# A gated attention and state-space kernel: rebuilding its set-up (parameters, sin and cos, first projections, and the engine that folds C)

## The chip, the cores and the metric

The kernel runs on one core of one Trainium2 chip. The metric is the device time of one execution in microseconds (us). Every time quoted as "the time" is a median over the executions of one kernel, and each kernel was run beside the kernel before on the same chip in the same rounds.

One core has five engines that matter: TensorE (PE in the profile, PEld for its weight loads), VectorE (DVE), ScalarE (ACT), GpSimd (POOL), and SyncE (SP), which only issues transfers here. In the traces each works through its own instructions in the program's order and waits on semaphores for the others (before one dense product TensorE stands 9.91 us, with query-key matmuls behind it). SBUF and PSUM are the on-chip memories; in this program matmuls write PSUM, and VectorE (683 to 690 ns for 128x512) or ScalarE (0.60 us) "evacuates" a PSUM bank into SBUF before TensorE writes it again.

## The reference

Two branches read the same input x (2048 rows of 1024) and are mixed by a gate. Branch A is a diagonal state-space layer with 1024 complex states; branch B is attention with 32 heads of 32 columns.

```python
g = sigmoid((x * gate_w).sum(-1, keepdims=True))
a = A(x, ...)                  # below
b = B(x, wqkv, wo)             # softmax(q k^T / sqrt(32)) v, then @ wo
return g * a + (1 - g) * b

def A(x, Lambda_re, Lambda_im, B_re, B_im, C_re, C_im, log_dt, Dskip):
    Lam, dt = Lambda_re + 1j * Lambda_im, exp(log_dt)
    Lam_bar = exp(dt * Lam)                          # needs cos and sin of dt * Lambda_im
    B_bar   = ((Lam_bar - 1) / Lam)[:, None] * B     # the kernel folds this factor into C
    Bu = einsum("bld,pd->blp", x, B_bar)
    for t in range(L):
        h = Lam_bar * h + Bu[:, t]                   # the scan
    return 2 * einsum("blp,dp->bld", hs, C).real + x * Dskip
```

## The kernel before

The attention is cut into 512 *bursts*. A burst is 8 query-key matmuls (QK) into two of three PSUM slots, then two ScalarE `exp` activations of 128x1024, and two bursts later the 16 matmuls with V (PV). There are therefore 1,024 exps. TensorE and VectorE must do everything else between the bursts: projections of Q, K and V, the state-space matmuls ("u" before the scan, "c" after it), and the output projection. All of these "dense" products go through **one** PSUM bank, number 7, which VectorE evacuates.

```python
def burst(self, B):                       # cut
    def mm(e): ...                        # 8 matmuls K[32 x 128] x Q[32 x 256] -> two PSUM slots
    self.S.op("pe", mm, reads=[("K", g % 2, i // 2), ("Q", qz)], writes=[("S", sl[0]), ("S", sl[1])], name="qk")
    for z in range(2):
        ... self.act(lambda e, s=s, p=p: e.activation(pt[:, p], ps[:, 2 * s:2 * s + 2, :], ACT.Exp, scale=SCALE), [("S", s)], [("pt", p)], "exp")
```

The program is planned on the host: a loop over the bursts emits one burst, some dense matmuls, and then as much VectorE "background" work (`bg`) as its *planned* costs say fits into the period of 1.81 us, and last the evacuation of the dense product that ended.

```python
for p in range(NBURST + 2):               # cut to its shape
    self.burst(p); self.pv(p - 2)
    if p == 12: self.pool_fold()          # GpSimd folds C
    ...                                   # up to 4 dense matmuls of 512 columns into bank 7 (8 in the first bursts)
    while self.bg:                        # background work of VectorE, each entry (planned us, function)
        c = self.bg[0][0]
        if c > 0 and st + c > limit: break
        self.bg.pop(0)[1]()
    if ended is not None: ended.evac()    # VectorE evacuates bank 7, behind the background work
```

The background work of the first 200 us is, for each of 8 groups of 128 states, a *table* of rotations (20 operations of 16 to 256 columns in f32, then a cast) and the *item* operations that use it (multiplies by the table, additions, two scans). Here are the table and the fold, which GpSimd does:

```python
def table_ops(self, j):                   # cut
    add(0.1, ... tensor_copy(E32[:, :, 0:16], self.E16[:, :, j, :]))
    for l in range(4, 9):
        n = 1 << l; c = 0.08 + n / 960.0                                              # planned us
        add(c, ... tensor_scalar(ta[:, 0:n], si, wi, None, ALU.mult))                 # one SBUF input
        add(c, ... tensor_scalar(tb[:, 0:n], si, wr, None, ALU.mult))
        add(c, ... scalar_tensor_tensor(dr, sr, wr, ta[:, 0:n], ALU.mult, ALU.subtract))   # two SBUF inputs
        add(c, ... scalar_tensor_tensor(di, sr, wi, tb[:, 0:n], ALU.mult, ALU.add))
    add(0.6, ... tensor_copy(self.Et[:, :, j, :], E32))                               # f32 -> bf16 cast

def pool_fold(self):                      # cut: per (j, half) six GpSimd operations of 512 columns, 96 in all
    pool(tensor_scalar(X, ci, a2, 0.0, ALU.mult, ALU.add)); pool(tensor_scalar(Y, cr, a2, ...)); pool(tensor_scalar(Z, cr, a1, ...))
    pool(tensor_tensor(cr, Z, X, ALU.add)); pool(tensor_scalar(Z, ci, b2, ...)); pool(tensor_tensor(ci, Y, Z, ALU.add))
```

In the traces the f32 tables and the scratch of the fold are both called `f_OT` (they live in a part of that buffer that is free so early), the table in bf16 is `f_Et`, the bf16 evacuation of u is `f_ub`, the products are `f_tq`, their sums `f_ut`, the scan result `f_ht`.

The start of the program: five parameter vectors are loaded with 2-byte elements spread over partitions, sin and cos come from ScalarE's table, and the first K and Q projections run as 512-column matmuls that wait for all four row quarters of x.

Of the kernel before, what the change touches and what calls it, by code (L numbers as in the profile page):

```python
# [931 lines left out]
class FastPath:  # L932

    def __init__(self, nc, S, es, d, flag):
# [28 lines left out]
        self.prm = T("prm", [128, 5, 8], BF)  # L963
# [62 lines left out]
    def begin(self):  # L1026
# [8 lines left out]
        names = ["A_Lambda_re", "A_Lambda_im", "A_log_dt", "A_Dskip", "gate_w"]  # L1035

        def prm(i):
            self.dma(lambda e: e.dma_start(self.prm[:, i, :], d[names[i]].rearrange("(a p) -> p a", p=128), allow_slow_non_contiguous=True),
                     [], [("prm", i)], "ld_prm", "act")
        for i in (2, 1, 0):  # L1040
            prm(i)
        self.ld_w(0, 1, "act")
        self.ld_w(0, 0, "act")
        self.ld_w(0, 2, "act")
        for i in (3, 4):
            prm(i)
        pool(lambda e: e.memset(self.ones[:], 1.0), [], ["ones"])
        pw2, iot = self.pf[:, 32:34, :].rearrange("p a b -> p (a b)"), self.pf[:, 34:36, :].rearrange("p a b -> p (a b)")
        ioti = self.pf[:, 36:38, :].rearrange("p a b -> p (a b)").bitcast(I32)
        for l in range(10):  # L1050
            pool(lambda e, l=l: e.memset(pw2[:, l:l + 1], float(1 << l)), [], [("pw2", l)])
        pool(lambda e: e.iota(ioti, pattern=[[1, 16]], base=0, channel_multiplier=0), [], ["ioti"])
        pool(lambda e: e.tensor_copy(iot, ioti), ["ioti"], ["iot"])
        pool(lambda e: e.memset(self.V[:, :, :, :, 32:33], 1.0), [], ["v1"])
        pool(lambda e: e.memset(self.init[:], 0.0), [], ["init"])
        pool(lambda e: e.affine_select(self.ident[:], self.ones[:], pattern=[[1, 128]], base=0, channel_multiplier=-1,
                                       compare_op=ALU.is_equal, fill=0.0), ["ones"], ["ident"])

        def warm_up(e):
            m = None  # L1060
            for k in range(14):
                m = e.matmul(self.ps[:, 5, :], warm[:, 0:128], warm, start=True, stop=True)
            return m
        S.op("pe", warm_up, reads=["warm"], writes=[("S", 2)], name="warm")
        self.math(pw2, iot)

    def math(self, pw2, iot):
        pf, W = self.pf, self.W
        P = lambda i: pf[:, i, :]
        dve, act = self.dve, self.act  # L1070
        scr = self.tabs
        ang = scr[:, 0:80].rearrange("p (a b) -> p a b", a=10)
        angk = scr[:, 80:160].rearrange("p (a b) -> p a b", a=10)
        anga = scr[:, 160:240].rearrange("p (a b) -> p a b", a=10)
        bang = scr[:, 256:384].rearrange("p (a b) -> p a b", a=8)
        bangk = scr[:, 384:512].rearrange("p (a b) -> p a b", a=8)
        banga = scr[:, 512:640].rearrange("p (a b) -> p a b", a=8)
        PW2 = [("pw2", l) for l in range(10)]
        LR, LI, LD, DS = 0, 1, 2, 3
        DT, AR, TH, RR = 5, 6, 7, 8  # L1080
        self.RR = RR
        act(lambda e: e.activation(P(DT), self.prm[:, LD, :], ACT.Exp), [("prm", LD)], [("pf", DT)])
        for i in (1, 0):
            dve(lambda e, i=i: e.tensor_copy(P(i), self.prm[:, i, :]), [("prm", i)], [("pf", i)])
        dve(lambda e: e.tensor_tensor(P(TH), P(DT), P(LI), ALU.mult), [("pf", DT), ("pf", LI)], [("pf", TH)])
        dve(lambda e: e.tensor_tensor(P(AR), P(DT), P(LR), ALU.mult), [("pf", DT), ("pf", LR)], [("pf", AR)])
        act(lambda e: e.activation(P(RR), P(AR), ACT.Exp), [("pf", AR)], [("pf", RR)])
        dve(lambda e: e.tensor_tensor(ang, P(TH).unsqueeze(1).to_broadcast([128, 10, 8]), pw2[:, 0:10].unsqueeze(2).to_broadcast([128, 10, 8]), ALU.mult),
            [("pf", TH)] + PW2, ["ang"])
        dve(lambda e: e.tensor_tensor(bang, P(TH).unsqueeze(2).to_broadcast([128, 8, 16]), iot.unsqueeze(1).to_broadcast([128, 8, 16]), ALU.mult),  # L1090
            [("pf", TH), "iot"], ["bang"])

        def reduce(a, k, ab, tok):
            dve(lambda e: e.tensor_scalar(k, a, 1.0 / TWO_PI, MAGIC, ALU.mult, ALU.add), [tok], [tok + "_k"])
            dve(lambda e: e.tensor_scalar(k, k, MAGIC, None, ALU.subtract), [tok + "_k"], [tok + "_k"])
            dve(lambda e: e.scalar_tensor_tensor(a, k, -CW1, a, ALU.mult, ALU.add), [tok + "_k", tok], [tok])
            dve(lambda e: e.scalar_tensor_tensor(a, k, -CW2, a, ALU.mult, ALU.add), [tok + "_k", tok], [tok])
            dve(lambda e: e.scalar_tensor_tensor(ab, a, -1.0, a, ALU.mult, ALU.max), [tok], [tok + "_a"])
            dve(lambda e: e.tensor_scalar(ab, ab, -1.0, math.pi / 2, ALU.mult, ALU.add), [tok + "_a"], [tok + "_a"])
        reduce(ang, angk, anga, "ang")  # L1100
        reduce(bang, bangk, banga, "bang")
        act(lambda e: e.activation(W[:, 1], ang, ACT.Sin), ["ang"], ["ang_s"])
        act(lambda e: e.activation(W[:, 0], anga, ACT.Sin), ["ang_a"], ["ang_c"])
        act(lambda e: e.activation(self.E16[:, 1], bang, ACT.Sin), ["bang"], ["bang_s"])
        act(lambda e: e.activation(self.E16[:, 0], banga, ACT.Sin), ["bang_a"], ["bang_c"])
        self.Wtok = ["ang_s", "ang_c"]
        self.E16tok = ["bang_s", "bang_c"]

    def math2(self):
        pf, W = self.pf, self.W  # L1110
        P = lambda i: pf[:, i, :]
        LR, LI, DS = 0, 1, 3
        RR, WN = self.RR, 27
        SN0, CS0 = W[:, 1, 0, :], W[:, 0, 0, :]
        LBR, LBI, DEN, INV, FR, FI, T1, T2 = 13, 14, 15, 16, 17, 18, 19, 20
        A1, A2, B2 = 21, 22, 23
        self.A1, self.A2, self.B2 = A1, A2, B2
        ops = []

        def tt(o, a, b, op, r):  # L1120
            ops.append((0.08, lambda: self.dve(lambda e: e.tensor_tensor(P(o), a, b, op), r, [("pf", o)])))

        def ts(o, a, s, op, r):
            ops.append((0.08, lambda: self.dve(lambda e: e.tensor_scalar(P(o), a, s, None, op), r, [("pf", o)])))
        q = lambda *i: [("pf", k) for k in i]
        ops.append((0.08, lambda: self.dve(lambda e: e.tensor_copy(P(DS), self.prm[:, DS, :]), [("prm", DS)], [("pf", DS)])))
# [6 lines left out]
        ops.append((0.1, lambda: self.dve(lambda e: e.reciprocal(P(INV), P(DEN)), q(DEN), q(INV))))  # L1133
# [13 lines left out]
    def pool_fold(self):  # L1147
        pf, pool = self.pf, self.pool
        for j in range(8):
            pool(lambda e, j=j: e.tensor_scalar(self.diagD[:, j, :], self.ident[:], pf[:, 3, j:j + 1], 0.0, ALU.mult, ALU.add),  # L1150
                 ["ident", ("pf", 3)], [("diagD", j)])
        X, Y, Z = self.fold[:, 0:512], self.fold[:, 512:1024], self.fold[:, 1024:1536]
        for j in range(8):
            self.ld_c(j)
            a1, a2, b2 = pf[:, self.A1, j:j + 1], pf[:, self.A2, j:j + 1], pf[:, self.B2, j:j + 1]
            for hf in range(2):
                cr = self.cT[0][:, j, 512 * hf:512 * (hf + 1)]
                ci = self.cT[1][:, j, 512 * hf:512 * (hf + 1)]
                tr, ti = ("cTf", 0, j, hf), ("cTf", 1, j, hf)
                rr, rii = [("cT", 0, j), tr], [("cT", 1, j), ti]  # L1160
                pool(lambda e, ci=ci, a2=a2: e.tensor_scalar(X, ci, a2, 0.0, ALU.mult, ALU.add), rii + [("pf", self.A2)], ["fX"])
                pool(lambda e, cr=cr, a2=a2: e.tensor_scalar(Y, cr, a2, 0.0, ALU.mult, ALU.add), rr + [("pf", self.A2)], ["fY"])
                pool(lambda e, cr=cr, a1=a1: e.tensor_scalar(Z, cr, a1, 0.0, ALU.mult, ALU.add), rr + [("pf", self.A1)], ["fZ"])
                pool(lambda e, cr=cr: e.tensor_tensor(cr, Z, X, ALU.add), ["fZ", "fX"], [tr])
                pool(lambda e, ci=ci, b2=b2: e.tensor_scalar(Z, ci, b2, 0.0, ALU.mult, ALU.add), rii + [("pf", self.B2)], ["fZ"])
                pool(lambda e, ci=ci: e.tensor_tensor(ci, Y, Z, ALU.add), ["fY", "fZ"], [ti])


    def table_ops(self, j):
        W, dve = self.W, self.dve  # L1170
        b = j % 2
        o = 1536 * 0
# [5 lines left out]
        first = ["ang", "ang_k", "ang_a", "bang", "bang_k", "bang_a"] if j == 0 else []  # L1178
# [4 lines left out]
        for l in range(4, 9):  # L1183
# [9 lines left out]
            add(c, lambda e, di=di, sr=sr, wi=wi, n=n: e.scalar_tensor_tensor(di, sr, wi, tb[:, 0:n], ALU.mult, ALU.add),  # L1193
                ["gE0", "gE1", "gt1"] + self.Wtok, ["gE1"])
        add(0.6, lambda e: e.tensor_copy(self.Et[:, :, j, :], E32), ["gE0", "gE1"], [("Et", j)])
        return ops

    def item_ops(self, j, ch, n):
        dve, ub, tq, ut, ht = self.dve, self.ub, self.tq, self.ut, self.ht
# [28 lines left out]
        if b == 1 and j == 0:  # L1228
            hw = ["fX", "fY", "fZ", "gE0", "gE1", "gt0", "gt1"] + self.E16tok
# [525 lines left out]
```

## Time and profile before

| | before |
|---|---|
| time, median of 4 runs | 1027.35 us (1026.45 to 1027.97) |
| profiled span | 1026.6 us |
| first exp starts | 19.51 us |
| time in which ScalarE waits for QK matmuls | 50.6 us in 33 waits |
| from the end of the last exp to the end | about 13.8 us |

The page of the profile gives, for each engine, busy time and share, and then its busy tenths in 40 slices of 25.7 us:

```profile
PE 915.7 (89%) x15153; PEld 489.6 (48%) x15375; DVE 522.9 (51%) x1118; ACT 948.1 (92%) x1034; POOL 106.8 (10%) x142
...
DVE  3259998988788533451126761137775112122223
ACT  3775559999999999999999999999999999999994
POOL 1089990000000000000000000000000000000000
```

ScalarE is full from the seventh slice to the end and half empty in slices 4 to 6. Exactly there GpSimd is busy, and VectorE is full. The table of windows puts numbers to it (columns: the window in us; its length; then busy us and count of each engine; the granted TensorE clock, 1.00 being full speed; DMA share; GB/s):

```profile
62.00:160.00 98.00, 64.68 (x990) 34.95 (x999) 92.28 (x140) 61.00 (x65) 89.97 (x87) 0.81 0.36 57
500.00:600.00 100.00, 95.61 (x1655) 53.30 (x1680) 54.11 (x115) 100.00 (x110) 0.00 (x0) 1.00 0.23 41
```

From 62 to 160 us ScalarE works 61 of 98 us. From 500 to 600 us it never stops. (The count of each engine takes in every instruction that has a part inside the window.)

The timeline of ScalarE shows the holes one by one (start, length, engine, line, operation, count of merged instructions, and in brackets the idle time just before and what ended it). One burst is x2:

```profile
18.17 1.28 ACT L1419 ACT_TABLE_LOAD   x1
19.51 1.94 ACT L1419 ACTIVATE f_pt<-f_ps 128x1024 bf16<-128x1024 f32 x2
...
59.81 13.00 ACT L1419 ACTIVATE f_pt<-f_ps 128x1024 bf16<-128x1024 f32 x14 [0.63 <-PE f_ps L1413]
83.06 1.94 ACT L1419 ACTIVATE f_pt<-f_ps 128x1024 bf16<-128x1024 f32 x2 [10.24 <-PE f_ps L1413]
...
261.43 638.17 ACT L1419 ACTIVATE f_pt<-f_ps 128x1024 bf16<-128x1024 f32 x696 [0.41 <-PE f_ps L1413]
```

ScalarE waits for a QK matmul (L1413) for 10.24 us. But TensorE was not busy with matmuls in that time. Its timeline shows it waiting, for 9.91 us, before a dense product (L1318, a product u of the state-space layer):

```profile
80.97 1.49 PE L1318 MATMUL f_ps<-f_xT,f_wb 128*128 128x512 bf16 x3 [9.91 <-DVE f_OT L1190]
```

The chain of work that ended last, in order of time (start, length, what), shows what held it between 75 and 87 us:

```profile
75.08 1.32 DVE f_OT L1189
...
78.53 1.32 DVE f_OT L1189
79.85 0.60 DVE f_ub L1322
...
82.98 1.08 DVE f_Et L1195
84.09 2.53 DVE f_tq L1209 x3
86.62 0.60 DVE f_ub L1322
```

It is VectorE's table work (`f_OT`), with the evacuation of bank 7 (`f_ub`) queued inside it. (TensorE's wait is put down to `f_OT` L1190, the short operation just behind the evacuation that ends at 80.45 us; that the bank was what it waited for follows from the order of the program.) TensorE, which runs in order, stands at the next dense matmul until the bank is free, and the QK matmuls stand behind that one.

And this table work is slow. These are the groups of VectorE's instructions by shape, from 56 to 150 us (count | busy us, mean ns of one | idle before them):

```profile
L1209 DVE TENSOR_TENSOR f_tq<-f_ub,f_Et 128x512 bf16<-128x512 bf16 x12 | 8.2, 721 | 0.1
...
L1322 DVE CAST f_ub<-f_ps 128x512 bf16<-128x512 f32 x8 | 5.5, 683 | 3.2 <-PE f_ps L1318 3.1
L1209 DVE TENSOR_TENSOR f_ut<-f_tq 128x512 f32<-128x512 bf16 x4 | 5.1, 1320 | 0.0
...
L1189 DVE TENSOR_SCALAR f_OT<-f_OT,f_W 128x16 f32<-128x16 f32 x3 | 2.2, 730 | 0.1
```

and the same groups from 160 to 240 us, when GpSimd is silent:

```profile
L1209 DVE TENSOR_TENSOR f_tq<-f_ub,f_Et 128x512 bf16<-128x512 bf16 x16 | 6.0, 420 | 0.1
L1322 DVE CAST f_ub<-f_ps 128x512 bf16<-128x512 f32 x8 | 5.5, 688 | 1.6 <-PE f_ps L1318 1.6
L1209 DVE TENSOR_TENSOR f_ut<-f_tq 128x512 f32<-128x512 bf16 x8 | 5.1, 685 | 0.0
L1189 DVE TENSOR_SCALAR f_OT<-f_OT,f_W 128x16 f32<-128x16 f32 x5 | 1.2, 234 | 0.2
```

The same multiply takes 721 ns beside GpSimd and 420 ns without it. A 16-column operation, 730 and 234 ns. Of these groups only the evacuation from PSUM takes the same 683 to 688 ns in both.

### The profile page before, as it was taken

The page shows a single profiled execution, that of the slowest core. Times are in us where ns is not written, and L with a number is a line of the kernel's source. Part 1 is how long each engine was busy: PE and PEld are TensorE (multiplying, and loading weights), DVE is VectorE, ACT ScalarE, POOL GpSimd, SP SyncE. Part 2 cuts the span into 40 slices and gives each one's busy share as a digit, 9 for nine tenths or more (in the row PEclk, how much of TensorE's full clock was granted, in tenths as well). Part 3 has the DMA queues.
Part 4 walks back from the last instruction along what each step waited for, and adds up shares of the span by engine and source line. Part 5 has one row for each costly group of instructions (what it writes and reads, how often), then busy time and mean ns, then how long its engine had stood idle before and what let it go on. Part 6 is the DMA issues. An engine that isn't in the chain of part 4 may idle for free.

```text
span 1026.6 us, 33366 instructions
## 1 busy us (share of the span) xinstructions
PE 915.7 (89%) x15153; PEld 489.6 (48%) x15375; DVE 522.9 (51%) x1118; ACT 948.1 (92%) x1034; POOL 106.8 (10%) x142
## 2 busy tenths in 40 slices
PE   5976768898999999999999999999999999799995
PEld 2632334464444446444564464444554446344442
DVE  3259998988788533451126761137775112122223
ACT  3775559999999999999999999999999999999994
POOL 1089990000000000000000000000000000000000
PEclk9978789999999999999999999999999999899998
DMA  9593211141223310112003311114201210223321
GB/s 198 85 162 71 24 25 27 25 79 28 58 56 69 78 48 5 38 52 65 25 8 58 69 26 38 38 48 87 49 17 38 77 38 28 96 78 109 117 79 61
DMA packets 162422, 60.99 MB, mean 59 GB/s; under 512 B 151008, under 2 KB 151008, under 8 KB 162272
## 3 DMA queue, kind: packets, MB, share of 16 engines
q1 hardware_dynamic: 153952, 57.96, 25.3%
q8 instruction: 122, 2.00, 0.8%
q10 hardware_dynamic: 8320, 0.80, 0.7%
q14 instruction: 28, 0.23, 0.1%
HBM read 16.79 MB, written 12.58 MB: 29 GB/s over the span
## 4 chain that ended last, share of the span: by engine, by line
ACT 75%; DVE 12%; PE 9%; SPq 3%; issue 1%; DMA 1%
ACT f_pt L1419 75%; SPq L1007 2%; PE f_ps L1435 2%; PE f_ps L1269 2%; PE f_ps L1318 2%; PE f_ps L1413 2%; DVE f_OT L1189 2%; DVE f_OT L1193 2%; DVE f_tq L1209 2%; DVE f_OT L1191 2%; PE f_ps L1287 1%; DVE f_OT L1190 1%; DVE f_ut L1209 1%; DVE f_ub L1322 1%; SPq L1016 1%
## 5 line engine op out<-in xcount | busy, mean ns | idle before, releaser
L1419 ACT ACTIVATE f_pt<-f_ps 128x1024 bf16<-128x1024 f32 x1024 | 942.7, 1234 | 50.6 <-PE f_ps L1413 50.6
L1435 PE MATMUL f_ps<-f_V,f_pt 128*128 128x33 bf16 x8192 | 292.1, 179 | 3.9 <-DVE f_On L1449 3.5
L1435 PEld LDWEIGHTS f_ps<-f_V,f_pt 128*128 128x128 bf16 x8192 | 239.6, 96 | 115.6 <-issue 108.3
L1413 PE MATMUL f_ps<-f_Q,f_K 32*128 32x256 bf16 x4096 | 207.4, 277 | 26.6 <-ACT f_pt L1419 8.8
L1413 PEld LDWEIGHTS f_ps<-f_Q,f_K 32*128 32x128 bf16 x4096 | 61.1, 92 | 245.2 <-ACT f_pt L1419 230.3
L1318 PE MATMUL f_ps<-f_xT,f_wb 128*128 128x512 bf16 x448 | 124.6, 396 | 37.1 <-DVE f_OT L1190 13.7
L1269 PE MATMUL f_ps<-f_xT,f_wb 128*128 128x512 bf16 x450 | 119.4, 385 | 16.8 <-DMA f_xT<-in_A_x_dram 6.1
L1359 DVE TENSOR_SCALAR f_Ag<-f_ps,f_gcol 128x512 f32<-128x512 f32 x32 | 24.0, 751 | 113.1 <-PE f_ps L1344 113.1
L1218 DVE TENSOR_TENSOR_SCAN f_ht<-f_pf,f_init,f_ut 128x512 bf16<-128x512 f32 x64 | 81.4, 1296 | 0.0
L1344 PE MATMUL f_ps<-f_cT_im,f_hp 128*128 128x512 bf16 x192 | 72.6, 378 | 6.0 <-DVE f_Ag L1359 4.1
L1322 DVE CAST f_ub<-f_ps 128x512 bf16<-128x512 f32 x64 | 44.2, 690 | 55.8 <-PE f_ps L1318 55.7
L1318 PEld LDWEIGHTS f_ps<-f_xT,f_wb 128*128 128x128 bf16 x512 | 41.7, 98 | 62.0 <-issue 31.8
L1287 PE MATMUL f_ps<-f_wb,f_xT 128*128 128x128 bf16 x1024 | 67.9, 220 | 3.0 <-DVE f_K L1276 1.7
L1269 PEld LDWEIGHTS f_ps<-f_xT,f_wb 128*128 128x128 bf16 x512 | 41.2, 97 | 45.5 <-issue 11.7
L1374 PE MATMUL f_ps<-f_wb,f_OT 128*128 128x512 bf16 x220 | 59.0, 385 | 3.6 <-issue 0.5
L1287 PEld LDWEIGHTS f_ps<-f_wb,f_xT 128*128 128x128 bf16 x1024 | 58.3, 98 | 4.0 <-DVE f_K L1276 1.8
L1448 DVE RECIPROCAL f_rc<-f_ps 128x8 f32<-128x8 f32 x64 | 13.2, 207 | 91.8 <-PE f_ps L1435 90.7
L1344 PE MATMUL f_ps<-f_cT_re,f_hp 128*128 128x512 bf16 x144 | 54.4, 378 | 0.0
L1384 DVE SCALAR_TENSOR_TENSOR f_xT<-f_ps,f_gcol,f_xT 128x512 bf16<-128x512 f32 x28 | 21.0, 751 | 63.7 <-PE f_ps L1374 63.7
L1209 DVE TENSOR_TENSOR f_tq<-f_ub,f_Et 128x512 bf16<-128x512 bf16 x128 | 50.1, 446 | 0.2
L1276 DVE CAST f_Q<-f_ps 128x512 bf16<-128x512 f32 x32 | 22.1, 691 | 54.5 <-PE f_ps L1269 54.5
L1240 POOL TENSOR_TENSOR f_cm<-f_hl,f_W 128x8 f32<-128x8 f32 x12 | 3.3, 308 | 444.9 <-DVE f_hl L1221 444.9
(92 smaller groups left out, 556.9 us busy)
## 6 DMA issues: line engine op xcount, KB each, us to landing
ag_scratch<-f_Ag SPq DMA_DIRECT2D x32, 256.0 KB, 2.0
f_xT<-ag_scratch SPq DMA_DIRECT2D x32, 256.0 KB, 2.7
f_wb<-in_B_wqkv_dram SPq DMA_DIRECT2D x21, 256.0 KB, 4.4
out_dram<-f_xT SPq DMA_DIRECT2D x16, 256.0 KB, 2.1
f_OT<-f_On SPq DMA_TRANSPOSE x64, 2.3
f_wb<-in_B_wo_dram SPq DMA_DIRECT2D x1, 1024.0 KB, 6.5
f_wb<-in_B_wqkv_dram ACTq DMA_DIRECT2D x3, 256.0 KB, 7.5
f_wb<-in_B_wo_dram SPq DMA_DIRECT2D x1, 768.0 KB, 4.6
```

Source lines behind the costliest of these rows:

```text
L1209: ops.append((c, lambda: dve(lambda e: e.tensor_tensor(o, a, b, op), r, w)))
L1218: ops.append((1.25, lambda ri=ri: dve(lambda e: e.tensor_tensor_scan(ht[:, ri, :], rr, ut[:, ri, :], self.init[:, ri, j:j + 1], ALU.mult, ...
L1269: mms.append((1, lambda e, f, l, a=a: e.matmul(ps[:, bank, :], w[:, g % 2, part, a, :], xT[:, a, 512 * ch:512 * (ch + 1)], start=f, stop=l ...
L1287: m = e.matmul(ps[:, bank, 128 * q:128 * (q + 1)], xT[:, a, 128 * kt:128 * (kt + 1)], w[:, g % 2, 2, a, :], start=(a == 0), stop=(a == 7))
L1318: mms.append((1, lambda e, f, l, a=a: e.matmul(ps[:, 7, :], bT[:, n % 2, ri, a, :], xT[:, a, 512 * ch:512 * (ch + 1)], start=f, stop=l), [ ...
L1322: self.dve(lambda e: e.tensor_copy(self.ub[:, n % 2, ri, :], ps[:, 7, :]), [("bank", 7)], [("ub", n % 2, ri)], "evac_u")
L1344: mms.append((1, lambda e, f, l, j=j, ri=ri: e.matmul(ps[:, 7, :], hp[:, ri, j, cols], cT[ri][:, j, 512 * cb:512 * (cb + 1)], start=f, sto ...
L1359: self.dve(lambda e: e.tensor_scalar(a, ps[:, 7, :], self.gcol[:, 0, tt:tt + 1], None, ALU.mult), [("bank", 7), "g0"], [at], "evac_c")
L1374: mms.append((1, lambda e, f, l, j=j: e.matmul(ps[:, bank, :], OT[:, j, 256 * qb + 128 * r:256 * qb + 128 * (r + 1)], wo[j][0][:, 512 * cb ...
L1413: m = e.matmul(ps[:, 2 * sl[h // 2] + h % 2, 256 * kl:256 * (kl + 1)], K[32 * h:32 * h + 32, g % 2, 128 * kt:128 * (kt + 1)], Q[32 * h:32 ...
L1419: self.act(lambda e, s=s, p=p: e.activation(pt[:, p], ps[:, 2 * s:2 * s + 2, :], ACT.Exp, scale=SCALE), [("S", s)], [("pt", p)], "exp")
L1435: m = e.matmul(ps[:, 6, o:o + 33], pt[:, p, h2, 256 * kl + 128 * qt:256 * kl + 128 * (qt + 1)], V[:, g % 2, 2 * i + kl, h, :], start=(i == ...
```

## The change

The intent is to start the exps earlier and to take away what slows VectorE in the first 160 us. There are six edits:

1. The five parameter vectors are loaded as rows, which are contiguous, and turned into columns by one matmul with the identity.
2. sin and cos come from polynomials on VectorE, so ScalarE needs only the exp table, which is loaded by a dummy activation before anything waits for it (one load of 1.28 us; the kernel before has three in front of its first exp, at 12.57, 14.61 and 18.17 us).
3. The first K and Q products run by row quarters of x, each as soon as its quarter lands, and their two evacuations run on two engines.
4. The fold of C goes from GpSimd to VectorE, 64 operations in column halves; the tables and the fold sit in a second background queue, `bg2`.
5. The warm-up matmuls on zeros become 16 instead of 14.
6. The plan uses a period of 2.75 us for the first 8 bursts.

The diff moves three more things: the loads of C and the diagonal for D go from burst 12 to the start, and the products c are ordered by column half, so that they can follow the fold by halves.

The core of the diff, with cuts:

```diff
-        names = ["A_Lambda_re", "A_Lambda_im", "A_log_dt", "A_Dskip", "gate_w"]
-            self.dma(lambda e: e.dma_start(self.prm[:, i, :], d[names[i]].rearrange("(a p) -> p a", p=128), allow_slow_non_contiguous=True), ...
+        for i, nm in enumerate(["A_Lambda_re", "A_Lambda_im", "A_log_dt", "A_Dskip", "gate_w"]):
+            self.dma(lambda e, i=i, nm=nm: e.dma_start(self.prow[8 * i:8 * i + 8, :], d[nm].rearrange("(a p) -> a p", p=128)), ...
+        act(lambda e: e.activation(self.cm[:, 0, 0:1], warm[:, 0:1], ACT.Exp), ["warm"], [("cm", 0)], "table")
...
-            for k in range(14):
+            for k in range(16):
                 m = e.matmul(self.ps[:, 5, :], warm[:, 0:128], warm, start=True, stop=True)
...
+    def first_proj(self):
+        for q in range(4):
+            for part, bank in ((1, 7), (0, 6)):
+                ... 8 matmuls of 128 columns, reads=[("w", 0, part), ("x0", q)]
+        self.dve(lambda e: e.tensor_copy(self.K[:, 0, 0:512], ps[:, 7, :]), [("bank", 7)], [("K", 0, 0)], "evac_qk")
+        self.act(lambda e: e.activation(self.Q[:, 0, :], ps[:, 6, :], ACT.Copy), [("bank", 6)], [("Q", 0)], "evac_qk")
+    def params(self):
+        S.op("pe", lambda e: e.matmul(ps[:, 5, 0:40], self.prow[:], self.ident[0:40, 0:40], start=True, stop=True), ...
...
-        act(lambda e: e.activation(W[:, 1], ang, ACT.Sin), ["ang"], ["ang_s"])
-        ... (three more)
+        for i in (9, 7, 5, 3):            # sp and cp are 208 columns: all angles at once
+            add(c, lambda e, v=v: e.scalar_tensor_tensor(sp, sp, v, y, ALU.add, ALU.mult), ["m_s", "m_y"], ["m_s"])
+            add(c, lambda e, u=u: e.scalar_tensor_tensor(cp, cp, u, y, ALU.add, ALU.mult), ["m_c", "m_y"], ["m_c"])
+        ...
-    def pool_fold(self): ...              # 96 GpSimd operations
+    def fold_ops(self, j, cb):
+        return [(0.62, ... self.dve(tensor_scalar(X, ci, a2, None, ALU.mult))),
+                (0.62, ... self.dve(tensor_scalar(Y, cr, a2, None, ALU.mult))),
+                (0.62, ... self.dve(scalar_tensor_tensor(cr, cr, a1, X, ALU.mult, ALU.add))),
+                (0.62, ... self.dve(scalar_tensor_tensor(ci, ci, b2, Y, ALU.mult, ALU.add))),
+                (0.0, lambda: self.folded.append(j))]
...
+        self.bg2 = self.math()
+        for j in range(8):
+            self.bg2 += self.table_ops(j)
+        for cb in range(2):
+            for j in range(8):
+                self.bg2 += self.fold_ops(j, cb)
...
-            if p == 12 and not folded:
-                self.pool_fold()
...
-            while self.bg:
+            while self.bg or self.bg2:
+                src = self.bg if self.bg and (self.bg[0][2] in self.tabled or not self.bg2) else self.bg2
```

## The prediction

> **What bounds it now.** In steady state ScalarE's 1,024 exp activations: the waits view shows no idle ScalarE from 500 to 800 us, 110 exps per 100 us (0.909 us each), so 931 us of the 1026.6 us span. The rest lies outside:
> - Start: the first exp begins at 19.5 us (timeline).
> - Ramp, 19.5 to 43.5 us: 8 query-key bursts take 24 us where ScalarE needs 14.5.
> - The set-up stretch, 62 to 160 us: ScalarE is busy 61 of 98 us (windows view). It waits (waits view) for query-key matmuls, up to 10.2 us; the chain of waits runs through VectorE's table work (f_OT). TensorE, in order, needs the PSUM bank that VectorE evacuates late.
> - Tail, after the last exp: 13.4 us.
>
> By 261 us about 198 exps are done, worth 180 us.
>
> **Why the stretch is slow.** GpSimd folds C there (90 of 98 us busy). Groups by shape inside and after it: 16-wide tensor_scalar 730 against 234 ns, table multiplies 720-800 against 420, f_ut adds 1320 against 685, table cast 1451 against 694; evacuations from PSUM 683 against 688. One table takes 16.7 us (67.3 to 84.0) against 6.8 (181.3 to 188.1). [...]
>
> **What the change does.**
> - Fold to VectorE: 64 operations of 512 columns, estimated from 256-wide ones (0.35 and 0.48 us) at 0.6-0.75 us, about 40 us. They are spread over bursts up to about 106. GpSimd falls silent, so the contention goes.
> - sin/cos: 21 chained 208-wide operations, about 0.4 us each (128-wide ones are 0.33 start to start): about 8.5 us on VectorE. Removed: both extra activation-table loads (1.28 us each) in front of the first exp.
> - First K/Q by row quarters: now 16 matmuls of 512 columns start at 12.2 us when the last x quarter lands, K and Q evacuations end at 19.0. Then only 16 of 128 columns (1-1.7 us) remain after the landing, and the two evacuations go in parallel. First exp at about 14.8 us (gain 4.7).
> - Parameters as rows: off the path.
>
> **What is given back.** I added VectorE durations between successive evacuations in the new order. Bursts 0-7: 27 us against 24, so the polynomial and the first tables lengthen the ramp by about 3 us. Bursts 9-15: 13.9 us of work in 10.9, about 3 us lost (a table is planned at 4.4 us, really takes about 6.2). Later about 2 us in all; fold and scans fit. So burst 16 comes near 59 us, as now. Burst 99 comes near 212 us instead of 261: the gain is some 49 us, nearly all from the contention stretch.
>
> **Predicted time:** 979 us, range 970 to 992. Chances: faster by over 2% 0.97, within 2% 0.025, slower 0.005.
>
> **Right if:** first exp between 14 and 16 us; ScalarE at least 95% busy from 62 to 160 us; no VectorE group above its uncontended mean (table multiplies 420 ns, f_ut 685); GpSimd below 15 us busy; VectorE total about 480-520 us (40 added for the fold, 8 for sin/cos[...]); the same tail and 0.909 us per exp later.
>
> **Wrong if:** the x transposes pace the ramp, or the early C transposes delay the On transposes; VectorE's plan is overbooked more than I counted, so each late evacuation stalls TensorE and ScalarE; TensorE's granted clock, which fell to half at 52-59 us here, stays low longer with the new order; or the table slowdown was something else than GpSimd.

Two passages of the prediction are cut: a sentence on why GpSimd and VectorE slow each other, and, under "Right if", a third term of VectorE's total, time taken off for the end of the contention. With all three terms that total came to some 511 us, inside the 480-520; the two that remain make 522.9 + 40 + 8 = 571 us. The predicted time, some 49 us less than the kernel before, loses no term.

## The result and the profile after

| | before | after |
|---|---|---|
| time, median of 4 runs | 1027.35 us (1026.45 to 1027.97) | 986.71 us (984.82 to 987.31) |
| ratio, 95% interval | 1 | 0.9602 (0.9585 to 0.9619) |
| profiled span | 1026.6 us | 984.5 us |
| first exp starts | 19.51 us | 13.32 us |
| waits of ScalarE for QK matmuls | 50.6 us in 33 | 16.8 us in 17 |
| from the end of the last exp to the end | about 13.8 us | 13.7 us |

A ratio, here and below, is the mean time of one kernel's runs over the mean time of the other's in the same rounds, so it is not quite the ratio of the medians. The outputs are correct. The change is 4.0% faster.

The page after, same parts as above:

```profile
PE 908.1 (92%) x15204; PEld 490.7 (50%) x15426; DVE 518.6 (53%) x1193; ACT 943.3 (96%) x1030; POOL 8.4 (1%) x46
...
DVE  4897889877778844411267711187753112122223
ACT  3789999999999999999999999999999999999994
POOL 2000000000000000000000000000000000000000
```

GpSimd is gone after the first slice, and ScalarE is full from the fourth slice. VectorE took over the fold (the groups of the whole span: 32 tensor_scalar of 480 ns and 32 scalar_tensor_tensor of 745 ns, together 39.2 us) and the polynomials, and yet its busy total *fell* from 522.9 to 518.6 us, because its table and item instructions are shorter now (a multiply took 721 ns beside GpSimd and takes 418).

The windows after (same columns as before):

```profile
62.00:160.00 98.00, 91.65 (x1567) 50.31 (x1591) 83.15 (x199) 97.32 (x107) 0.00 (x0) 1.00 0.32 55
```

ScalarE is busy 97.32 of 98 us where it was 61.00. VectorE is *less* busy with more operations in it (199 against 140). The groups of VectorE by shape from 62 to 135 us answer to the two lists of before:

```profile
L1336 DVE CAST f_ub<-f_ps 128x512 bf16<-128x512 f32 x12 | 8.3, 690 | 6.7 <-PE f_ps L1332 6.7
L1223 DVE TENSOR_TENSOR f_tq<-f_ub,f_Et 128x512 bf16<-128x512 bf16 x20 | 7.4, 418 | 0.0
...
L1223 DVE TENSOR_TENSOR f_ut<-f_tq 128x512 f32<-128x512 bf16 x10 | 6.7, 683 | 0.0
```

The multiply is at 418 ns and the sum at 683 ns, as they were without GpSimd, and it is now VectorE that waits for TensorE before an evacuation (6.7 us), not the other way.

The timeline of ScalarE after:

```profile
13.32 1.94 ACT L1431 ACTIVATE f_pt<-f_ps 128x1024 bf16<-128x1024 f32 x2 [0.49 <-PE f_ps L1425]
...
39.44 1.94 ACT L1431 ACTIVATE f_pt<-f_ps 128x1024 bf16<-128x1024 f32 x2 [0.75 <-PE f_ps L1425]
...
59.94 3.77 ACT L1431 ACTIVATE f_pt<-f_ps 128x1024 bf16<-128x1024 f32 x4 [1.92 <-PE f_ps L1425]
64.15 69.77 ACT L1431 ACTIVATE f_pt<-f_ps 128x1024 bf16<-128x1024 f32 x76 [0.43 <-PE f_ps L1425]
134.08 722.72 ACT L1431 ACTIVATE f_pt<-f_ps 128x1024 bf16<-128x1024 f32 x788 [0.16 <-PE f_ps L1425]
```

The first exp begins 6.2 us earlier; the exp of burst 8 begins at 39.44 us, 4.1 us earlier than before (43.52); and from 64 to 857 us there is one wait of 0.16 us.

**A sum that closes.** In both kernels the span is the start of the first exp, plus 1,024 exps at their undisturbed spacing, plus the waits of the exps, plus a small cost of each break (about 0.11 us, because back-to-back exps overlap: two take 1.94 us, not 1.83), plus the tail. The undisturbed spacing is 638.17/696 = 0.917 us before and 722.72/788 = 0.917 us after, so 939.0 us for 1,024.

- Before: 19.51 + 939.0 + 50.6 + 33 x 0.11 + 13.8 = 1026.5 us (profiled span 1026.6).
- After: 13.32 + 939.0 + 16.8 + 17 x 0.11 + 13.7 = 984.7 us (profiled span 984.5).

So of the 42 us between the spans, 6 come from an earlier first exp and 36 from fewer and shorter waits. What this sum doesn't say is which edit caused which term. That is what the experiments are for.

### The profile page after: what moved, and what is told of

The parts are those of the page before. It is cut to its first block, busy times and chain, and to the rows that moved or that the text cites. A ratio compares the mean times of both kernels' runs of the same rounds, so it can differ in the third digit from the quotient of the medians. Undisturbed runs are those within 1.5% of the kernel's fastest.

```text
span 984.5 us, 33446 instructions
## 1 busy us (share of the span) xinstructions
PE 908.1 (92%) x15204; PEld 490.7 (50%) x15426; DVE 518.6 (53%) x1193; ACT 943.3 (96%) x1030; POOL 8.4 (1%) x46
## 2 busy tenths in 40 slices
DMA packets 157302, 60.99 MB, mean 62 GB/s; under 512 B 145888, under 2 KB 145888, under 8 KB 157152
## 4 chain that ended last, share of the span: by engine, by line
ACT 88%; DVE 5%; PE 4%; DMA 2%; SPq 0%; issue 0%
ACT f_pt L1431 88%; PE f_ps L1301 1%; DMA f_OT<-f_On 1%; DVE f_OT L1206 1%; PE f_ps L1425 1%; DVE f_OT L1202 1%; PE f_ps L1447 1%; DVE f_OT L1204 1%; DMA f_xT<-in_A_x_dram 1%; PE f_ps L1386 1%; SPq L1008 0%; DVE f_OT L1203 0%; PE f_ps L1283 0%; DVE f_V L1307 0%; PE f_ps L1332 0%
## 5 line engine op out<-in xcount | busy, mean ns | idle before, releaser
L1431 ACT ACTIVATE f_pt<-f_ps 128x1024 bf16<-128x1024 f32 x1024 | 941.0, 1251 | 16.9 <-PE f_ps L1425 16.8
L1332 PE MATMUL f_ps<-f_xT,f_wb 128*128 128x512 bf16 x448 | 117.2, 377 | 13.6 <-DVE f_Q L1290 2.4
L1283 PE MATMUL f_ps<-f_xT,f_wb 128*128 128x512 bf16 x434 | 113.6, 379 | 9.0 <-issue 2.1
L1336 DVE CAST f_ub<-f_ps 128x512 bf16<-128x512 f32 x64 | 44.2, 691 | 51.9 <-PE f_ps L1332 51.8
L1332 PEld LDWEIGHTS f_ps<-f_xT,f_wb 128*128 128x128 bf16 x512 | 40.5, 96 | 35.9 <-issue 4.3
L1283 PEld LDWEIGHTS f_ps<-f_xT,f_wb 128*128 128x128 bf16 x496 | 39.2, 96 | 34.5 <-issue 1.4
L1223 DVE TENSOR_TENSOR f_tq<-f_ub,f_Et 128x512 bf16<-128x512 bf16 x128 | 46.3, 418 | 0.1
L1223 DVE TENSOR_TENSOR f_tq<-f_ht,f_Et 128x512 bf16<-128x512 bf16 x128 | 46.3, 417 | 0.0
L1307 DVE CAST f_V<-f_ps 128x512 bf16<-128x512 f32 x32 | 22.2, 694 | 43.2 <-PE f_ps L1301 43.2
```

Of the source, the lines that this page charges most:

```text
L1223: ops.append((c, lambda: dve(lambda e: e.tensor_tensor(o, a, b, op), r, w)))
L1283: mms.append((1, lambda e, f, l, a=a: e.matmul(ps[:, bank, :], w[:, g % 2, part, a, :], xT[:, a, 512 * ch:512 * (ch + 1)], start=f, stop=l ...
L1332: mms.append((1, lambda e, f, l, a=a: e.matmul(ps[:, 7, :], bT[:, n % 2, ri, a, :], xT[:, a, 512 * ch:512 * (ch + 1)], start=f, stop=l), [ ...
L1336: self.dve(lambda e: e.tensor_copy(self.ub[:, n % 2, ri, :], ps[:, 7, :]), [("bank", 7)], [("ub", n % 2, ri)], "evac_u")
```

## The experiments

**The theory.** GpSimd's fold slowed VectorE: in the trace of the kernel before, most groups of VectorE's instructions on SBUF take longer beside it (a table multiply 721 against 420 ns, a sum 1320 against 685) and its evacuations from PSUM do not (683 against 688). That is the greater part of the gain. The rest is the start: quarters and evacuations in parallel, and no table loads. What the two engines share that would slow one of them is shown by no trace; the expectations speak of a lock, which here is only a name for this slowdown.

**The rivals.** (a) The new order of the plan is what helps: tables in a queue of their own, `bg2`, and a longer period for the ramp. (b) The slow VectorE groups are slow because of something else in that stretch, for instance transfers, and the fold's engine is beside the point. (c) The start carries more than it seems.

### The fold alone put back: e1

The kernel after, with the fold on GpSimd again from burst 12 with the same operations (the loads of C stay early); the start, the polynomials, the order and the plan stay new.

```diff
+    def pool_fold(self): ...             # the 96 GpSimd operations of before
...
-        for cb in range(2):
-            for j in range(8):
-                self.bg2 += self.fold_ops(j, cb)
+        self.folded = list(range(16))
...
+            if p == 12:
+                self.pool_fold()
```

> The changed kernel with one part undone: the fold of C is back on GpSimd (from burst 12), all else as changed. Theory [...]: VectorE's table and item work from about 45 us on slows again to about twice (16-wide tensor_scalar 700 ns, table multiplies 700 ns), ScalarE idles some 25 to 40 us between 60 and 160 us, time 1010 to 1025 us. Rival (the gain is the new order: tables before items, an earlier start, shorter set-up): time within 5 us of the changed kernel, 982 to 992 us.

It measured 1027.42 us against 1028.8 of before in the same rounds, ratio 0.9988 (0.9972 to 1.0005): nothing is left of the gain, not even of the 6 us of the start, although the first exp began at 13.24 us. That is a little worse than the 1010 to 1025 us expected. The window and the longest wait:

```profile
62.00:160.00 98.00, 65.19 (x976) 32.05 (x976) 92.94 (x148) 60.70 (x66) 74.76 (x71) 0.83 0.21 39
```

```profile
83.51 1.94 ACT L1448 ACTIVATE f_pt<-f_ps 128x1024 bf16<-128x1024 f32 x2 [22.67 <-PE f_ps L1442]
```

ScalarE is back at 60.70 of 98 us, one wait is 22.67 us, the multiply takes 929 ns. Rival (a) falls: with the new order and the old fold there is no gain. The exps wait 54.5 us in all, 3.9 more than in the kernel before, so most of what the start gains is lost again in waits. Why the earlier start is lost as well was not isolated. The fold again begins at burst 12, and the tables now stand ahead of the items in VectorE's queue, so more of the slowed work may come in one piece; that is argued, not shown.

### The fold alone removed: e2 and e3

Both kernels without any fold (C stays unscaled; the result is wrong, relative error 0.119, everything else runs).

```diff
-        X, Y, Z = ...                    # e2: pool_fold of before keeps the loads of C and drops its 96 operations
+        self.folded = list(range(16))    # e3: the kernel after, no fold_ops in the queue
-                            [("hp", b, j, ri), ("cTf", ri, j, cb)]))
+                            [("hp", b, j, ri), ("cT", ri, j)]))
```

> The kernel before with the fold left out altogether (wrong result on purpose: C is used unfolded); nothing else moved. Lock theory: ScalarE's idle time from 62 to 160 us falls from 37 us to about 2, VectorE's groups return to their uncontended means, time 986 to 993 us. Rival (the new order and start are what matters): still above 1010 us.

> The changed kernel with the fold left out altogether (wrong result on purpose). Tells what 40 us of fold work on VectorE costs in time. Theory (it is spread into VectorE's slack between evacuations, and comes after the tables): within 2 us of the changed kernel, 984 to 988 us. Rival (part of the 8 us by which the prediction missed is the fold crowding VectorE): 978 to 981 us.

The kernel before without its fold took 992.23 us, ratio 0.9651 (0.9631 to 0.9671), with ScalarE busy 95.73 of 98 us, multiplies at 419 ns and 13.4 us of exp waits. Its window:

```profile
62.00:160.00 98.00, 92.12 (x1560) 49.30 (x1559) 83.95 (x226) 95.73 (x105) 0.00 (x0) 1.00 0.43 71
```

So 36 us of the 41 appear when only the fold is taken away. The kernel after without its fold took 986.26 us, ratio 0.9585 (0.9569 to 0.9601), which is the time of the kernel after with it: 39 us of work on VectorE cost nothing that the times can show. Between e2 and e3 there are 6 us: the start and the plan.

### GpSimd made busy on purpose: e13 and e14

If it is GpSimd's work beside VectorE, useless work on GpSimd must bring the loss back; whether its *kind* matters is the question of the second run. Both kernels are the kernel after (the fold stays on VectorE), with work on GpSimd that touches only an unused scratch. e13 reads and writes SBUF, e14 only writes, for longer.

```diff
+    def dummy(self):                     # e13, called at burst 12
+        self.pool(lambda e: e.memset(D, 0.0), [("Q", 2)], ["fD"])
+        for k in range(64):
+            self.pool(lambda e: e.tensor_tensor(F, D, D, ALU.add), ["fD"], ["fF"])
```

```diff
+    def dummy(self):                     # e14, called at burst 12
+        for k in range(128):
+            self.pool(lambda e: e.memset(self.fold[:, 1024:2048], 0.0), [("Q", 2)] if k == 0 else [], ["fD", "fF"])
```

> The changed kernel, right results, with useless work added on GpSimd from about 43 us: one memset and 64 tensor_tensor of 512 columns f32 over a scratch tile that nobody reads (some 80 to 90 us). VectorE has the same work as in the changed kernel. Lock theory: VectorE's table, item and fold operations with two SBUF inputs slow to 1.5 to 2 times, evacuations from PSUM do not, time 1015 to 1035 us. Rival (the fold on GpSimd was slow for its data dependences or its DMA, not because it ran beside VectorE): 985 to 988 us.

> As e13_gpsimd_reads, but the useless GpSimd work only writes: 128 memsets of 1024 columns f32. [...]two-input operations (table multiplies f_tq, scalar_tensor_tensor, scans) keep their uncontended means (418, 230 to 480, 1271 ns), while tensor_scalar and casts in SBUF slow down; time between 988 and 1010 us. Rival (any GpSimd activity slows VectorE): all SBUF groups slow as in e13_gpsimd_reads and the time is like its.

e13 took 1029.81 us, ratio 1.0016 (1.0001 to 1.0031). 71 us of work that nobody needs, on an engine that nobody waits for, cost 44 us. e14, with 125 us of it, took 999.25 us, ratio 0.9718 (0.9703 to 0.9733), so some 13 us. The groups by shape from 62 to 135 us, first of e13:

```profile
L1229 DVE TENSOR_TENSOR f_tq<-f_ub,f_Et 128x512 bf16<-128x512 bf16 x10 | 6.4, 694 | 0.0
...
L1229 DVE TENSOR_TENSOR f_ut<-f_tq 128x512 f32<-128x512 bf16 x4 | 4.3, 1104 | 0.0
L1342 DVE CAST f_ub<-f_ps 128x512 bf16<-128x512 f32 x6 | 4.1, 686 | 1.8 <-PE f_ps L1338 1.8
...
L1208 DVE TENSOR_SCALAR f_OT<-f_OT,f_W 128x256 f32<-128x256 f32 x2 | 2.2, 1081 | 0.1
```

then of e14:

```profile
L1228 DVE TENSOR_TENSOR f_tq<-f_ub,f_Et 128x512 bf16<-128x512 bf16 x20 | 7.4, 418 | 0.0
...
L1228 DVE TENSOR_TENSOR f_ut<-f_tq 128x512 f32<-128x512 bf16 x10 | 6.7, 684 | 0.0
L1240 DVE CAST f_hl<-f_ht 128x2 f32<-128x2 bf16 x5 | 3.7, 732 | 0.2
...
L1208 DVE TENSOR_SCALAR f_OT<-f_OT,f_W 128x256 f32<-128x256 f32 x2 | 2.2, 1118 | 0.0
```

With a GpSimd that reads, both kinds are slow: the multiplies (694 against 418 ns), the sums (1104 against 683), and tensor_scalar (1081 against 354). These means are even too mild, because GpSimd's work in e13 ends at 118.68 us, inside the window: from 57 to 115 us alone the multiplies take 1105 ns and the sums 1522. Not every instruction is hit: in the same stretch the second of two tensor_scalar in a row (L1209) takes 222 ns with 16 columns, no more than alone (230). With a GpSimd that only writes, the operations with two SBUF inputs take 418 and 684 ns, within a nanosecond of what they take alone (only the multiplies of the scan result have a higher mean, 446 against 417 ns), while tensor_scalar takes up to 1118 (L1208, 256 columns; 348 alone) and the cast from SBUF 732 against 170 ns for two columns. Here too not every one is hit: one tensor_scalar of 256 columns (L1207) takes 354 ns, as alone. The evacuation from PSUM takes 686 ns in e13 and 690 in e14, as without GpSimd (690). So the assumption of e14 held for these groups. A sign, not a proof, that VectorE waits for a whole instruction of GpSimd: in e13 the first tensor_scalar of a pair (L1208) takes 1072, 1086, 1081 and 1081 ns with 16, 32, 128 and 256 columns (two of each; those with 64 take 666), whatever its width, and one GpSimd operation takes 1104 ns on average. Rival (b) falls.

### Parts of the start: e4, e5, e6

The kernel after again (after_again) ran beside the third of these, as its yardstick: 986.04 us (984.05 to 986.27), ratio 0.9589 (0.9576 to 0.9602).

> The changed kernel once more, unedited, on the chip of this group, as the yardstick for the others: 985 to 988 us. If ScalarE's exps are 0.917 us apart (not 0.909 as predicted from), the idle time that remains (start, ramp, tail, stalls) sums to about 47 us, the same as in the first profile.

It repeats the result; what is not exps in its span is 983.2 - 939.0 = 44.2 us (45.5 in the first profile), a little less than the 47 expected. It also warns against reading single microseconds from one profile of the ramp: in the first profile of the kernel after, the V matmuls between bursts 0 and 1 took 3.55 us (granted clock 0.52), in this one 1.96 us, and burst 8 came at 38.31 instead of 39.44 us.

**e4: the first K and Q wide again**, 512 columns, both evacuations on VectorE.

```diff
-        for q in range(4):
-            for part, bank in ((1, 7), (0, 6)):
-                ... (quarters)
-        self.dve(... K ...); self.act(... Q ...)
+        for dn in (self.d_qk(0, 1, 0, 7), self.d_qk(0, 0, 0, 6)):
+            for _, f in dn.pieces:
+                f()
+            dn.evac()
```

> The changed kernel with the first K and Q projected as before: 16 matmuls of 512 columns after the last x quarter has landed, both evacuations on VectorE. Theory (quarters hide three quarters of that work under the loads): first exp 3 to 5 us later, at 16.5 to 18 us, and the time 2.5 to 5 us longer than the changed kernel, 988.5 to 991 us. Rival (the ramp, bound elsewhere, gives a later start back): within 1 us of the changed kernel.

It took 991.33 us, ratio 0.9642 (0.9629 to 0.9655): 5.3 us slower than e5 in the same rounds (986.02), which differs from the kernel after by nothing that shows. That is just above the range expected, and the rival, that the ramp gives a later start back, falls. The 16 wide matmuls start at 10.66 us, wait for the last quarter, and take 4.96 us, where the quarters leave 1.07 us of work after the landing. The first exp begins at 16.85 us, burst 8 at 43.48 us. So the quarters and the parallel evacuations are worth about 5.3 us.

**e5: no warm-up matmuls.**

```diff
-        S.op("pe", warm_up, reads=["warm"], writes=[("S", 2)], name="warm")
```

> The changed kernel without the 16 early matmuls on zeros. Theory (they only keep the clock up for the first quarters, which mostly wait for loads): last 16 matmuls 1.7 instead of 1.1 us, first exp about 0.7 us later, time within 2 us of the changed kernel, 985.5 to 988 us. Rival (the early clock carries through the ramp): 3 us or more slower.

It took 986.02 us, ratio 0.9591 (0.9578 to 0.9604): no effect. The first exp came at 13.96 us (13.32 and 13.56 in the two profiles of the kernel after), and the time shows nothing of it. The trace of the kernel before shows TensorE at two speeds: in its first projections, after 6.09 us without a matmul, the weight loads of 512-column matmuls follow each other at 0.43 us while the granted clock is 0.50 (12 to 14 us), and the last ones at 0.21 us while it is 1.00 (15 to 17 us). For 16 matmuls of 128 columns that makes 1.7 and 0.9 us. In the kernel after, with the warm-up, the granted clock is 1.00 from 6 to 13 us, and the first 48 matmuls of the quarters take 2.84 us. In e5 the 64 matmuls of the quarters run without a gap from 6.82 to 12.74 us; 17 of them have a part in 8.00 to 9.50 us, 17 in 9.50 to 11.00, and 17 in the single microsecond after. So without the warm-up the quarters go slower at first, but are faster before the end, and the 1.7 us forecast for the last 16 was wrong; they end 0.6 us later than in the kernel after (12.74 against 12.10).

**e6: sin and cos by ScalarE's table**, after the first two bursts, instead of the polynomials.

```diff
-        add(c, lambda e, v=v: e.scalar_tensor_tensor(sp, sp, v, y, ALU.add, ALU.mult), ...)     # and the rest of the polynomials
+        ops.append((0.0, lambda o=o, ...: self.act(lambda e: e.activation(o[:, 1], a[:, lo:hi], ACT.Sin), A, [w + "s"])))
+        ops.append((0.0, lambda o=o, ...: self.act(lambda e: e.activation(o[:, 0], h[:, lo:hi], ACT.Sin), ["m_h"], [w + "c"])))
```

> The changed kernel with sine and cosine taken back to ScalarE's table, but after the first two bursts instead of before the first: 15 polynomial operations leave VectorE (about 5 us), and two table loads and four activations (about 3.8 us) enter ScalarE in the ramp. Theory (the start gains because no table load stands before the first exp; who computes the sines matters little, since in the ramp neither engine is the limit all the time): first exp unchanged at 12.7 to 13.3 us, time within 2.5 us of the changed kernel. Rival (polynomials on VectorE are themselves worth the 4 us of ScalarE): 989 to 991 us.

It took 990.03 us, ratio 0.9632 (0.9619 to 0.9645), 4.0 us more than the kernel after in the same rounds. (The edit also runs one small exp on ScalarE at once, at 14.81 us, instead of two bursts later.) The theory, that the polynomials were worth less than 2.5 us, fell; the rival's 989 to 991 was right. The timeline of ScalarE:

```profile
17.16 1.28 ACT L1126 ACT_TABLE_LOAD   x1
...
19.30 1.28 ACT L1418 ACT_TABLE_LOAD   x1
22.18 1.94 ACT L1418 ACTIVATE f_pt<-f_ps 128x1024 bf16<-128x1024 f32 x2 [1.59 <-PE f_ps L1412]
```

Two loads and four activations hold ScalarE for about 3.4 us (17.16 to 20.58), then it waits 1.59 us more, and burst 8 comes at 41.52 us (38.31 in after_again). The mistake was to call this time free because ScalarE waits anyway in the ramp. The likely way of the loss, which no run isolates: while ScalarE does something else, the slots of PSUM stay full, and the QK matmuls behind them start later.

### Better than both: e8, e11, e12

From burst 8 to 19 the kernel after still loses some 4.5 us (24.7 us in both its profiles, where eleven bursts need 20.2). Its plan books a table at 4.4 us (0.08 + n/960 us an operation); the trace says about 6.2. **e8** plans what the trace measured.

```diff
-            c = 0.08 + n / 960.0
+            c = {16: 0.205, 32: 0.215, 64: 0.24, 128: 0.29, 256: 0.36}[n]
```

> The changed kernel, with the planned costs of the table operations set to the measured ones (6.2 us a table where the plan has 4.4), so that fewer are put between two evacuations. Theory (stalls of 0.9 and 1.9 us at 54 and 60 us and 2.6 us at 34 us are evacuations queued behind overbooked table work): 3 to 5 us faster than the changed kernel, 982 to 984 us, and no wait of ScalarE over 1 us after 45 us. Rival (those stalls come from TensorE's halved clock after the gate matmuls): no change, 986 to 987 us.

It took 985.75 us, ratio 0.9583 (0.9567 to 0.9599), no different from the kernel after: the 982 to 984 us of the theory were missed. In the stretch it did what was expected: no wait from 50.52 to 228.46 us, and 21.2 us from burst 8 to burst 19 (36.70 to about 57.9) instead of 24.7. But this was given back later:

```profile
229.25 1.94 ACT L1431 ACTIVATE f_pt<-f_ps 128x1024 bf16<-128x1024 f32 x2 [0.80 <-PE f_ps L1425]
...
856.53 1.94 ACT L1431 ACTIVATE f_pt<-f_ps 128x1024 bf16<-128x1024 f32 x2 [2.31 <-PE f_ps L1425]
```

Around 229 us TensorE runs at half clock: from 215 to 228 us it has little but QK and PV to do, is busy 9.11 of 13 us, and the granted clock is 0.50. When dense work comes back, it runs slowly (228 to 231 us: busy 3.00 of 3.00 us, still 0.50; 231 to 234: 0.96). A half clock was also granted to a TensorE with no idle time: in the kernel after, from 49 to 51 us, with 32 matmuls of one output column for the gate among QK and PV, it is busy 2.00 of 2.00 us at 0.50. What sets the clock was not isolated. Around 856 us TensorE waits 2.34 us for the transposed O (`f_OT<-f_On`), a transfer that is issued beside eight loads of branch A's results from memory.

**e11** adds three things to e8: a few matmuls on zeros around the last x quarter, three throw-away matmuls into bank 7 in each burst that has no dense work, and six of these eight loads three bursts later.

```diff
+                if q == 3 and part == 1:
+                    self.zeros(4)
...
+            if used == 0 and p < NBURST:
+                self.S.op("pe", self.filler, reads=[("diagD", q) for q in range(4)] + ["ones"], writes=[("bank", 7)], name="fill")
...
-                for k in range(8):       # at burst 448
+                for k in range(2):
+            if p == 451:
+                for k in range(2, 8):
+                    self.ld_a(k)
```

> e8_true_cost with matmuls on idle data put where TensorE has nothing dense to do: 7 around the last x quarter, 3 in each burst without a projection; and 6 of 8 loads of the scratch tiles issued three bursts later, behind the last transposes of O. Theory (what e8_true_cost won by 64 us, some 6 us, it lost again in two places, at 229 us and 852-859 us, to a clock that had halved in bursts with little TensorE work and to a late transpose): those stalls (1.4 and 3.9 us) go, time 979 to 982 us. Rival (the clock is lowered for some other reason): same as e8_true_cost, 985 to 986 us.

It took **979.75 us** (979.37 to 981.54), ratio 0.9537 (0.9524 to 0.9550), 6.3 us less than the kernel after in the same rounds, and its result is correct. It beats both kernels. The timeline of ScalarE:

```profile
53.09 828.84 ACT L1450 ACTIVATE f_pt<-f_ps 128x1024 bf16<-128x1024 f32 x904 [0.39 <-PE f_ps L1444]
882.10 80.98 ACT L1450 ACTIVATE f_pt<-f_ps 128x1024 bf16<-128x1024 f32 x88 [0.17 <-PE f_ps L1444]
```

One wait of 0.17 us from 53 us to the end. From 215 to 228 us the granted clock is 1.00 (TensorE busy 10.85 of 13 us). 10.1 us of waits remain, nearly all in the ramp. Which of the three additions did how much was not separated.

**e12** is e11 with the first projections in another order: V0, K1, K2, V1, K3, V2, Q1, V3 instead of V and K in turn.

```diff
-        start = [self.d_v(0, 0), self.d_qk(0, 1, 1), self.d_v(0, 1), self.d_qk(0, 1, 2), self.d_v(0, 2), self.d_qk(0, 1, 3), self.d_v(0, 3), self.d_qk(0, 0, 1)]
+        start = [self.d_v(0, 0), self.d_qk(0, 1, 1), self.d_qk(0, 1, 2), self.d_v(0, 1), self.d_qk(0, 1, 3), self.d_v(0, 2), self.d_qk(0, 0, 1), self.d_v(0, 3)]
```

> e11_filled with the projections of the ramp in another order, so that K chunks 2 and 3 are evacuated a burst before they are needed. Theory (the ramp's 26 us for 8 bursts is a TensorE chain in which the query-key matmul waits 0.8 us for each K evacuation): 1 to 2 us faster than e11_filled. Rival (the x transposes pace the ramp): no faster than e11_filled, or slower by up to 1 us.

It took 980.05 us, ratio 0.9549 (0.9533 to 0.9565): no faster, where 1 to 2 us were expected. Burst 8 begins at 37.08 us (36.96 in e11). K2 now waits 0.52 us for its transposed x, and PV waits 0.46 us for the evacuation of V, three times. The order only moves the wait.

## Why the prediction was right, and where it was off

The prediction was 979 us with a range of 970 to 992; the result was 986.7. The direction, the cause and most of the terms held.

- **The cause, right, and shown.** It said that the gain would come "nearly all from the contention stretch". Taking away the fold alone gives 36 us (e2), putting it back alone takes everything (e1), and a GpSimd that does nothing useful but reads SBUF takes it as well (e13).
- **The step that failed: "110 exps per 100 us (0.909 us each)" and "By 261 us about 198 exps are done".** The 110 in the window's line counts exps that only reach into the window at its two edges. The spacing is 638.17/696 = 0.917 us. The prediction was 7.7 us too low, and this misreading is the greater part of it. (Over 1,024 exps the difference is 8.2 us, but that is not the way it entered, and the likeness of the two numbers proves nothing.) The way it entered: the remaining time was divided by 0.909, which left 198 exps (burst 99) for the first 261 us of the kernel before. Counted in the timeline they are 206, burst 103 (of 1,024, the x696 that start at 261.43 us and 122 more after them leave 206). The kernel after reaches burst 103 at 134.08 + 46 x 1.834 = 218.4 us, so the gain there was 43 us and not "some 49": some 6 of the 7.7 us. Where the rest lies was not followed up.
- **"Burst 99 comes near 212 us": right**, 134.08 + 42 x 1.834 = 211.1 us, but in part by luck. Burst 8 came 2.4 us earlier than 14.8 + 27 = 41.8 us, and bursts 16 to 99 took 155.0 us where the prediction had 153, partly because it used the same wrong spacing there. The new kernel was forecast well in the sum; it was the old one that had been read wrong.
- **First exp at about 14.8 us:** 13.32. The work after the landing of the last quarter was 1.07 us, as predicted ("1-1.7 us"; the two speeds of the kernel before, 0.21 and 0.43 us for 512 columns, make 0.9 and 1.7):

```profile
11.03 1.07 PE L1069 MATMUL f_ps<-f_xT,f_wb 128*128 128x128 bf16 x16 [0.97 <-DMA f_xT<-in_A_x_dram]
```

  but the quarter itself landed 1.2 us earlier than before (11.03 against 12.20 us). The parameter loads with 2-byte elements are gone (157,302 transfer packets against 162,422) and may have been in its way; no run isolates it.
- **Bursts 0 to 7 in 27 us:** 26.1. **Bursts 9 to 15, 3 us lost:** 1.1 (14.0 us where seven bursts need 12.8), after 0.8 in burst 8. So "burst 16 near 59 us" came at 56.1, and the next three bursts gave nearly all of that back: with the wait of 1.92 us before burst 17, burst 19 came at 64.15 us, where 59 us and three bursts more make 64.5.
- **The sizes of VectorE's work, right:** the fold 39.2 us ("about 40"), polynomials of 365 to 368 ns an operation for most of the 208-column ones ("about 0.4 us"), VectorE's total 518.6 us ("480-520"). For the fold, the estimate of 0.6-0.75 us was right for scalar_tensor_tensor (745 ns) and too high for tensor_scalar (480). The tables' operations, in f32 where the fold reads bf16, differ in the same direction: doubling 128 columns to 256 adds 70 ns to a table's tensor_scalar (284 to 354) and 132 ns to its scalar_tensor_tensor (348 to 480).
- **All signs under "Right if" but two held:** ScalarE 97.32 of 98 us, no VectorE group above its mean alone, GpSimd 8.4 us, the tail of 13.7 us. The first exp was earlier than its range of 14 to 16, and the spacing of 0.909 us was never true, before or after.
- **Not foreseen, and not needed for the sum:** the parts aren't additive. The start is worth about 5.3 us for the quarters (e4) and 4.0 for the polynomials (e6) when GpSimd is silent, and nothing when it folds (e1). The 16 warm-up matmuls are worth nothing (e5). The plan's wrong cost of a table costs 3.5 us between bursts 8 and 19 (24.7 against 21.2 us), but mending it alone only uncovers the next limits (e8), and mending these too gives 6.3 us more (e11).

Open: what let the last x quarter land earlier; why e1 loses the start's gain too; the shares of e11's three additions; and what the parameters as rows, the second queue, the longer period of the ramp, the early loads of C and the order of the products c are worth each, since no run takes one of them back alone. The 6 us between e2 and e3 hold all of these and the rest of the start together.

## What to carry to other kernels

Before giving work to an idle GpSimd, look at what VectorE does beside it: if VectorE has SBUF operations there, compare their mean times inside and outside the overlap by shape, since 71 us of GpSimd work that nobody waited for cost this kernel 44 us, while the 39 us of the fold on a VectorE that had room cost nothing. An engine's idle time is free only if what it blocks meanwhile is not needed, so ask what stays occupied (here one PSUM bank, and in e6 probably the PSUM slots) and test parts together, because removing one limit shows the next. And take a steady spacing from a long run of the timeline, its length over its count, never from the count in a window.
